# Ten closing transfers regrouped into seven in a decode layer bound by loads

## The chip, the cores and the metric

The kernel runs on one core of one Trainium2 chip. The metric is device microseconds of one execution, the median of the runs shown. A profiled execution gives the trace, all of whose times are microseconds from the start of its span.

## The reference

One token of width D = 640 goes through attention over a cache of 8192 positions in 32 heads of width 192, and then a gated feed-forward layer of width 1536. All numbers are float32. Cut to what matters:

```python
def _A_ref(x, k_cache, v_cache, wq, wo):
    q = (x @ wq).reshape(B, Sq, H, Dh)                      # heads in front
    scores = jnp.einsum("bhqd,bhkd->bhqk", q, k_cache) * (Dh ** -0.5)
    p = _softmax(scores, axis=-1)
    o = jnp.einsum("bhqk,bhkd->bhqd", p, v_cache)
    return o.reshape(B, Sq, H * Dh) @ wo

def _B_ref(x, W_gate, W_up, W_down):
    gate, up = x @ W_gate, x @ W_up
    gate = gate * (gate > 0)
    return (gate * up) @ W_down

h = x + _A_ref(_layernorm(x), k_cache, v_cache, wq, wo)
out = h + _B_ref(_layernorm(h), W_gate, W_up, W_down)
```

## The kernel before

**Layout.** The host packs the inputs so that each transfer is one long row for each of 128 partitions. `kk[h]` is one head's K: 12288 columns of 4 bytes (`KW`). `vv[h]` is one head's V in twelve blocks of 1024 columns, then that head's output weights (960 columns, `WO`), then the next head's query weights (960 columns, `WQ`); 14208 columns in all (`VW`). The last head's V and output weights, without query weights, are `v0`. The feed-forward weights are `ww`: up (7680 columns), gate (7680) and down (7680).

On the chip one tensor, `big`, holds a single K buffer `kt`, two V buffers `vts[0]` and `vts[1]`, and the five columns of x. The feed-forward weights are laid over K and the first V buffer, starting at column 0, once those are free.

**Order of the loads.** All large loads are issued by SP (`sync_fn`), on one queue that the sixteen DMA engines drain in order. For each head, K (line 133) waits for the semaphore `sp`, counted when the scores of the head before are done. V (line 138) waits for `wo`, counted when the output projection that reads the buffer is done. The two then alternate in a loop. The last head is written out by hand: K in two halves with semaphores `k` and `k2`, V in two pieces (line 154), seven blocks on `vb` and five blocks with the output weights on `vb1`. Then come waits for `wo` and `sp` of the last head, and six feed-forward pieces (line 158), cut at the columns in `CUTS`: up; three fifths of gate; the rest of gate with two of down's twelve blocks; six blocks; three blocks; one block.

**One head.** In `tensor_fn`, TensorE computes the query (five pairs of matmuls over the query weights), waits for K, and computes the scores with 24 matmuls for each half of K: the program's 12 float32 matmuls are each two in the trace. A wait for `k2` stands between the halves. For all heads but the last SP raises `k2` ahead of time. Then `output` projects the head before, whose V is already weighted. VectorE takes the maximum of the scores, ScalarE the exponential, TensorE the sums (tile `pl`), VectorE their reciprocal. After that VectorE multiplies the twelve V blocks by the weights and sums them, one custom operation of 1024 columns each (line 126); in the second head of each loop pass it waits for `vb1` before block number `JV` = 7. In the middle of the twelve it also extracts the next query's two columns.

**The end.** `tensor_end` projects the last head, and the layer norm of the sum gives `hc`, the operand of up and gate. `project` runs up (40 traced matmuls) and gate (40), all into tile `sp`. Before gate's fourth block of rows it runs an idle matmul of 256 columns that computes nothing used. ScalarE scales up's result, VectorE multiplies it with the positive part of gate and transposes it (`guT`), while TensorE runs two more idle matmuls. Then come the 96 traced matmuls of down, into `pq`, a copy by ScalarE (line 340), and two small stores. `weights` puts a wait for a piece's semaphore in front of the first matmul that reads at one of the cuts.

Of the kernel before, what the change touches and what calls it, by code (L numbers as in the profile page):

```python
# [10 lines left out]
P, Q, NQ = 128, 32, 4  # L11
H, S, DH, D, F = 32, 8192, 192, 640, 1536
DJ, FJ = D // P, F // P
NG = 8
C = P // NG
SG = S // NG
NJ = DH // C
QB = 512
# [3 lines left out]
DG, FG, HN = D // NQ, F // NQ, D // 2  # L22
KW = S + S // 2
WO = D + HN
WQ = DJ * DH
VW = KW + WO + WQ
JV = 7
GATE, DOWN, FW = DJ * F, 2 * DJ * F, 2 * DJ * F + FJ * D
CUTS = (0, GATE, GATE + 3 * F, DOWN + 2 * D, DOWN + 8 * D, DOWN + 11 * D, FW)
SCALE = DH ** -0.5  # L30
EPS = 1e-5

# [24 lines left out]


def mha_decode_reglu_kernel(nc, x, w0, kk, vv, v0, ww, out):
    names = ("xr", "k", "k2", "va", "vb", "vb1", "qd", "qs", "sp", "mp", "pt", "m1", "rs",  # L60
             "pl", "q", "op", "po", "o", "o2", "wo", "cst", "st", "ffn0", "ffn1", "ffn2", "ffn3", "ffn4",
             "ffn5", "h4", "hm", "hc", "hr", "pu", "us", "pg", "gu", "pd", "pool", "dve")
    stored, s_o4 = (nc.alloc_semaphore("e_" + n) for n in ("out", "o4"))
    s = {n: nc.alloc_semaphore("e_" + n) for n in names}
    nums = sorted(x.num for x in s.values())
# [2 lines left out]
    def sb(name, shape):  # L68
        return nc.alloc_sbuf_tensor(name, shape, F32).ap()
# [1 line left out]
    def ps(name, shape):  # L71
        return nc.alloc_psum_tensor(name, shape, F32).ap()

    big = sb("big", [P, KW + 2 * VW + DJ])
    kt, vt2 = big[:, 0:KW], big[:, KW:]
    vts = [vt2[:, i * VW:(i + 1) * VW] for i in range(2)]
    xrow = sb("xrow", [NQ, DG])
    quad = sb("quad", [NQ, P])
    ones = sb("ones", [P, P])
# [40 lines left out]
    po = ps("po", [P, QB])  # L120
    acc = ps("acc", [P, QB])

    xT = vt2[:, 2 * VW:2 * VW + DJ]

    def ttr(eng, dst, a, b, scale, res):
        return eng.tensor_tensor_reduce(out=res, in0=a, in1=b, scale=scale, scalar=0.0,  # L126
                                        op0=ALU.mult, op1=ALU.add, accum_out=dst)

    def sync_fn(sy):
        def load_k(h, n, dst=kt, c=slice(0, KW), sem="k"):  # L130
            if n is not None:
                sy.wait_ge(s["sp"], n)
            sy.dma_start(dst[:, c], kk[h][:, c]).then_inc(s[sem], 16)  # L133

        def load_v(h, n, b):
            if n is not None:
                sy.wait_ge(s["wo"], n)
            sy.dma_start(vts[b], vv[h]).then_inc(s["vb" if b else "va"], 16)

        sy.dma_start(vt2[:, VW + KW + WO:2 * VW + DJ], w0).then_inc(s["vb"], 16)  # L140
        load_k(0, None)
        load_v(0, None, 0)
        sy.sem_inc(s["k2"], 16 * (H - 1))
        sy.sem_inc(s["vb1"], 16 * (H // 2))
        with sy.Fori(1, H - 2, 2) as i:
            load_k(i, i)
            load_v(i, i, 1)
            load_k(i + 1, i + 1)
            load_v(i + 1, i + 1, 0)
        load_k(H - 1, H - 1, c=slice(0, KW // 2))  # L150
        load_k(H - 1, None, c=slice(KW // 2, KW), sem="k2")
        sy.wait_ge(s["wo"], H - 1)
        for c0, c1, n in ((0, JV * SG, "vb"), (JV * SG, KW + WO, "vb1")):
            sy.dma_start(vts[1][:, c0:c1], v0[:, c0:c1]).then_inc(s[n], 16)
        sy.wait_ge(s["wo"], H)
        sy.wait_ge(s["sp"], H)
        for i, (c0, c1) in enumerate(zip(CUTS, CUTS[1:])):
            sy.dma_start(big[:, c0:c1], ww[:, c0:c1]).then_inc(s[f"ffn{i}"], 16)  # L158

    def store(eng, g):  # L160
        rows = out[0].rearrange("o (g n) -> (o g) n", g=NQ)
# [181 lines left out]
    def mm(dst, lhsT, rhs, start, stop, **kw):  # L343
        return nc.tensor.matmul(dst, lhsT, rhs, start=start, stop=stop, **kw)  # L344

    def weights(c0, n):
        if c0 in CUTS:
            nc.tensor.wait_ge(s[f"ffn{CUTS.index(c0)}"], 16)
        return big[:, c0:c0 + n]

    def project(c0, w0, done):
        for j in range(DJ):
            if w0 + j * F == CUTS[2]:
                idle(QB // 2)
            for g in range(NQ):
                ins = mm(sp[g * Q:(g + 1) * Q, c0:c0 + FG], hc[:, j, :], weights(w0 + j * F + g * FG, FG),
                         j == 0, j == DJ - 1)
            if j == 0 and c0 == 0:
                nc.tensor.wait_ge(s["st"], 8)
                mm(pl[:, 0:1], ones, st[:, 10:11], True, True).then_inc(s["st"])  # L360
        ins.then_inc(s[done])
# [15 lines left out]
    def tensor_fn(t):  # L377
        def query(w):
            wq = w.rearrange("p (j n) -> p j n", n=DH)
            for j in range(DJ):  # L380
                ins = mm(pq[:, 0:DH], xn[:, j:j + 1].to_broadcast([P, P]), wq[:, j, :], j == 0, j == DJ - 1)
            ins.then_inc(s["q"])

        def scores():
            for u in range(NU):
                if u:
                    yield
                for k in range(3):
                    for g in range(NQ):
                        c0 = u * (KW // 2) + (k * NQ + g) * QB  # L390
                        ins = mm(sp[g * Q:(g + 1) * Q, u * QB:(u + 1) * QB], qs[:, k, :], kt[:, c0:c0 + QB],
                                 k == 0, k == 2)
            ins.then_inc(s["sp"])
            yield

        def head(i, b, i8):
            n = i + b if b else i
            t.wait_ge(s["va" if b else "vb"], i8)
            query(vts[1 - b][:, KW + WO:VW])
            t.wait_ge(s["qs"], n)  # L400
            sc = scores()
            k_wait(i, b, "k")
            next(sc)
            k_wait(i, b, "k2")
            next(sc)
            output(t, n, vts[1 - b])
            t.wait_ge(s["mp"], n)
            t.transpose(pt[:, 0:P], mp.to_broadcast([P, P]), ident).then_inc(s["pt"])  # L408
            t.wait_ge(s["rs"], n)
            mm(pl[:, 0:1], share, rs, True, True).then_inc(s["pl"])  # L410

        def k_wait(i, b, name):
            t.wait_ge(s[name], i * 16 + 16 * b if b else i * 16)

        t.wait_ge(s["op"], 1)
        t.wait_ge(s["st"], 1)
        mm(pt[:, 0:1], ones, st[:, 4:5], True, True).then_inc(s["st"])
        t.wait_ge(s["xr"], 16)
        mm(acc[:, 0:DG], quad, xrow, True, False, skip_group_check=True)
        t.wait_ge(s["st"], 3)  # L420
        mm(pl[:, 0:1], ones, st[:, 6:7], True, True).then_inc(s["st"])
        t.wait_ge(s["st"], 7)
        with t.Fori(1, H + 1, 2) as i:
            i8 = i * 8 + 8
            head(i, 0, i8)
            head(i, 1, i8)
        t.sem_inc(s["q"], 1)

    def idle(n):
        mm(pt[:, 0:n], ident, p[:, 0:n], True, True)  # L430

    def tensor_end(t):
        output(t, H + 1, vts[1])
        t.wait_ge(s["h4"], 1)
        mm(pt[:, 0:1], ones, hs1, True, True).then_inc(s["hm"])

        t.wait_ge(s["hc"], 1)
        project(0, 0, "pu")
        project(QB, GATE, "pg")
        idle(QB)  # L440
        idle(QB // 2)
        for g in range(NQ):
            mm(pq[g * Q:(g + 1) * Q, 0:DG], ones[g * Q:g * Q + 1, 0:Q], h4[g * Q:g * Q + 1, :], True, False,
               skip_group_check=True)
        t.wait_ge(s["gu"], 1)
        for j in range(FJ):
            for g in range(NQ):
                ins = mm(pq[g * Q:(g + 1) * Q, 0:DG], guT[:, j, :], weights(DOWN + j * D + g * DG, DG),
                         False, j == FJ - 1, skip_group_check=True)
        ins.then_inc(s["pd"])  # L450
# [14 lines left out]
def _pack(x, k, v, wq, wo, up, gate, down):  # L465

    import numpy as _np

    kk = _np.empty((H, P, KW), k.dtype)
    vv = _np.empty((H - 1, P, VW), v.dtype)  # L470
    v0 = _np.empty((P, KW + WO), v.dtype)
    w0 = _np.empty((P, WQ + DJ), v.dtype)
    w = wq.reshape(P, DJ, H, DH)
    o = wo.reshape(H, DH, D)
    w0[:, 0:WQ] = w[:, :, 0, :].reshape(P, WQ)
    w0[:, WQ:] = x.reshape(P, DJ)
    for h in range(H):
        t = k[0, h].T
        kh = kk[h].reshape(P, NU, 3, NQ, QB)
        kh[:, :, 0:2] = t[0:D1].reshape(P, NQ, 2, NU, QB).transpose(0, 3, 2, 1, 4)  # L480
        kh[:, :, 2] = t[D1:].reshape(D2, NQ, 2, NU, QB).transpose(2, 0, 3, 1, 4).reshape(P, NU, NQ, QB)
        r = vv[h] if h < H - 1 else v0
        r[:, 0:KW] = v[0, h].reshape(NG, SG, NJ, C).transpose(0, 3, 2, 1).reshape(P, KW)
        r[:, KW:KW + D] = o[h, 0:D1]
        r[:, KW + D:KW + WO] = o[h, D1:].reshape(D2, 2, HN).transpose(1, 0, 2).reshape(P, HN)
        if h < H - 1:
            r[:, KW + WO:] = w[:, :, h + 1, :].reshape(P, WQ)
    ww = _np.concatenate([a.reshape(P, -1) for a in (up, gate, down)], axis=1)
    return w0, kk, vv, v0, ww


# [21 lines left out]
```

## Time and profile before

| What | Value |
|---|---|
| Median of 3 runs | 1038.33 us (1038.3 to 1038.48) |
| The profiled execution | 1038.14 us |
| Its span, first to last instruction | 1036.9 us |
| TensorE matmuls / VectorE busy | 438.0 us (42%) / 525.2 us (51%) |
| Bytes moved, rate | 445.98 MB, 430 GB/s |
| Mean granted TensorE clock | 0.641 |

A row of a timeline gives the start, the busy time, the engine and line, the operation, the tiles it writes and reads, and in brackets how long the engine had been idle and what released it. Rows that merge several instructions end in their number. The chain of waits is followed back from the last instruction: each row is a stretch of work or a transfer on which the next one waited. A row of windows gives the stretch, its length, TensorE's busy time, its granted clock, the DMA engines' mean busy share and the rate.

### The profile page before, as it was taken

The page shows a single profiled execution, that of the slowest core. Times are in us where ns is not written, and L with a number is a line of the kernel's source. Part 1 is how long each engine was busy: PE and PEld are TensorE (multiplying, and loading weights), DVE is VectorE, ACT ScalarE, POOL GpSimd, SP SyncE. Part 2 cuts the span into 40 slices and gives each one's busy share as a digit, 9 for nine tenths or more (in the row PEclk, how much of TensorE's full clock was granted, in tenths as well). Part 3 has the DMA queues.
Part 4 walks back from the last instruction along what each step waited for, and adds up shares of the span by engine and source line. Part 5 has one row for each costly group of instructions (what it writes and reads, how often), then busy time and mean ns, then how long its engine had stood idle before and what let it go on. Part 6 is the DMA issues. An engine that isn't in the chain of part 4 may idle for free.

```text
span 1036.9 us, 7438 instructions
## 1 busy us (share of the span) xinstructions
PE 438.0 (42%) x2746; PEld 201.2 (19%) x2746; DVE 525.2 (51%) x1162; ACT 74.5 (7%) x174; POOL 2.8 (0%) x18
## 2 busy tenths in 40 slices
PE   4255343344443344443443443443433553433536
PEld 2122121122121121111221111221211221211203
DVE  1644465644555544556544556444656444656472
ACT  1000000000000000000000000000000000000001
POOL 1000000000000000000000000000000000000000
PEclk8566666666655666655666655666656666656667
DMA  9999999999999999999999999999999999999998
GB/s 402 450 423 432 432 427 449 420 428 432 434 449 420 449 430 432 432 420 451 419 432 432 431 449 420 427 434 436 446 420 451 423 432 432 424 451 420 427 435 346
DMA packets 10532, 445.98 MB, mean 430 GB/s; under 512 B 1176, under 2 KB 1184, under 8 KB 1568
## 3 DMA queue, kind: packets, MB, share of 16 engines
q1 hardware_dynamic: 10516, 445.92, 99.6%
q8 instruction: 3, 0.05, 0.0%
q14 instruction: 1, 0.01, 0.0%
q10 hardware_dynamic: 12, 0.00, 0.0%
HBM read 445.91 MB, written 0.00 MB: 430 GB/s over the span
## 4 chain that ended last, share of the span: by engine, by line
DMA 76%; PE 23%; issue 0%; SPq 0%; DVE 0%; ACT 0%
DMA big<-in_kk_dram 72%; PE sp L344 23%; DMA big<-in_ww_dram 3%; SPq L133 0%; SPq L158 0%; PE pq L344 0%; PE acc L344 0%; SPq L140 0%; DVE junk L126 0%; PE po L344 0%; ACT o L340 0%; DVE o L126 0%
## 5 line engine op out<-in xcount | busy, mean ns | idle before, releaser
L126 DVE CUSTOM_DVE_ANT_0 big<-big,p 128x1024 f32<-128x1024 f32 x384 | 444.9, 1220 | 146.5 <-DMA big<-in_vv_dram 145.3
L344 PE MATMUL sp<-big,qs 128*32 128x512 f32 x1536 | 239.9, 789 | 342.9 <-DMA big<-in_kk_dram 338.4
L344 PE MATMUL pq<-big,xn 128*128 128x192 f32 x320 | 113.4, 540 | 154.2 <-DMA big<-in_vv_dram 152.3
L344 PEld LDWEIGHTS sp<-big,qs 128*32 128x32 f32 x1536 | 55.9, 140 | 513.4 <-DMA big<-in_kk_dram 359.7
L126 DVE CUSTOM_DVE_ANT_0 junk<-blk,po,rl 128x8 f32<-128x8 f32 x66 | 11.9, 218 | 265.5 <-PE po L344 265.5
L344 PEld LDWEIGHTS pq<-big,xn 128*128 128x128 f32 x320 | 97.9, 331 | 157.0 <-DMA big<-in_vv_dram 155.0
L303 ACT ACTIVATE o<-side,o 128x64 f32<-128x64 f32 x33 | 11.5, 348 | 479.2 <-DVE o L126 479.2
L315 ACT ACTIVATE qs<-pick,q 128x64 f32<-128x64 f32 x33 | 11.5, 348 | 410.3 <-DVE q L126 410.3
L321 ACT ACTIVATE p<-sp,m 128x1024 f32<-128x1024 f32 x32 | 35.6, 1113 | 47.9 <-DVE m L259 47.9
L257 DVE TENSOR_REDUCE mp<-sp 128x1 f32<-128x1024 f32 x32 | 39.0, 1220 | 0.0
L344 PE MATMUL pl<-rs,share 128*128 128x1 f32 x64 | 16.5, 327 | 51.9 <-ACT p L321 51.9
L261 DVE RECIPROCAL rl<-pl 128x1 f32<-128x1 f32 x32 | 5.4, 169 | 59.0 <-PE pl L344 59.0
L344 PE MATMUL acc<-big,o 128*32 128x160 f32 x528 | 28.8, 316 | 15.3 <-DVE o L126 15.3
L126 DVE DVE_READ_ACCUMULATOR2_ANT op<- 128x1 f32 x384 | 31.4, 82 | 0.0
L344 PEld LDWEIGHTS pl<-rs,share 128*128 128x128 f32 x64 | 13.8, 268 | 58.0 <-ACT p L321 58.0
L344 PE MATMUL po<-op,same 128*128 128x12 f32 x66 | 13.1, 272 | 16.0 <-PEq L452 16.0
L344 PEld LDWEIGHTS po<-op,same 128*128 128x128 f32 x66 | 10.0, 191 | 42.9 <-issue 26.8
L259 DVE TENSOR_REDUCE m<-pt 128x1 f32<-128x128 f32 x32 | 9.3, 292 | 13.3 <-PE pt L408 13.3
L344 PEld LDWEIGHTS acc<-big,o 128*32 128x32 f32 x528 | 10.6, 108 | 25.8 <-DVE o L126 18.4
L408 PE MATMUL pt<-ident,mp 128*128 128x128 f32 x32 | 10.3, 323 | 8.9 <-DVE mp L257 8.9
L126 DVE CUSTOM_DVE_ANT_0 junk<-ident,pq 128x128 f32<-128x128 f32 x33 | 9.3, 282 | 3.7 <-PE pq L344 3.7
L316 ACT ACTIVATE qs<-pick,q 128x32 f32<-128x32 f32 x33 | 10.1, 307 | 0.0
(78 smaller groups left out, 73.8 us busy)
## 6 DMA issues: line engine op xcount, KB each, us to landing
big<-in_vv_dram SPq DMA_DIRECT2D x31, 7104.0 KB, 38.8
big<-in_kk_dram SPq DMA_DIRECT2D x31, 6144.0 KB, 23.6
big<-in_kk_dram SPq DMA_DIRECT2D x2, 3072.0 KB, 19.5
big<-in_ww_dram SPq DMA_DIRECT2D x1, 3840.0 KB, 20.3
big<-in_v_dram SPq DMA_DIRECT2D x1, 3584.0 KB, 30.2
big<-in_v_dram SPq DMA_DIRECT2D x1, 3040.0 KB, 37.1
big<-in_ww_dram SPq DMA_DIRECT2D x1, 2304.0 KB, 25.5
big<-in_ww_dram SPq DMA_DIRECT2D x1, 2176.0 KB, 30.2
```

The source lines that it names most:

```text
L126: return eng.tensor_tensor_reduce(out=res, in0=a, in1=b, scale=scale, scalar=0.0, op0=ALU.mult, op1=ALU.add, accum_out=dst)
L257: v.reduce_max(mp, sp, axis=AX.X).then_inc(s["mp"])
L259: v.reduce_max(m1, pt[:, 0:P], axis=AX.X, negate=True).then_inc(s["m1"])
L261: v.reciprocal(rl, pl[:, 0:1])
L303: a.mul(o2, side, o[:, 1:2]).then_inc(s["o2"])
L315: a.mul(qs[:, 0:2, :], pk[:, 0:2, :], q[:, 0:1])
L316: a.mul(qs[:, 2, :], pk[:, 2, :], q[:, 1:2]).then_inc(s["qs"])
L321: a.activation(p, sp, AF.Exp, bias=m1, accum_out=rs).then_inc(s["rs"])
L344: return nc.tensor.matmul(dst, lhsT, rhs, start=start, stop=stop, **kw)
L408: t.transpose(pt[:, 0:P], mp.to_broadcast([P, P]), ident).then_inc(s["pt"])
```

## The change

The last head's K comes whole, on `k`; `k2` and its waits are gone from every head. V's first piece is ten blocks. Its second piece, on `vb1`, is two blocks, the output weights and all of up, and it is issued after a wait for the last head's scores, since its columns reach into K's place. For that the buffers change places in `big`: V1, the columns of x padded to 16, K, V0. What is left of the feed-forward weights comes in four pieces, placed behind up, over the rest of K and over V0: gate with two down blocks; six blocks; three; one. The idle matmul inside `project` is gone. The bytes in total are the same.

```diff
-JV = 7
-GATE, DOWN, FW = DJ * F, 2 * DJ * F, 2 * DJ * F + FJ * D
-CUTS = (0, GATE, GATE + 3 * F, DOWN + 2 * D, DOWN + 8 * D, DOWN + 11 * D, FW)
+JV = 10
+XW = 16
+UP = DJ * F
+VL = KW + WO + UP
+GATE, DOWN, FW = 0, DJ * F, DJ * F + FJ * D
+CUTS = (0, DOWN + 2 * D, DOWN + 8 * D, DOWN + 11 * D, FW)
...
-    big = sb("big", [P, KW + 2 * VW + DJ])
-    kt, vt2 = big[:, 0:KW], big[:, KW:]
-    vts = [vt2[:, i * VW:(i + 1) * VW] for i in range(2)]
+    big = sb("big", [P, VW + XW + KW + VW])
+    xT, kt = big[:, VW:VW + DJ], big[:, VW + XW:VW + XW + KW]
+    vts = [big[:, VW + XW + KW:], big[:, 0:VW]]
+    upw, ffn = big[:, KW + WO:VL], big[:, VL:VL + FW]
...
-        sy.sem_inc(s["k2"], 16 * (H - 1))
...
-        load_k(H - 1, H - 1, c=slice(0, KW // 2))
-        load_k(H - 1, None, c=slice(KW // 2, KW), sem="k2")
+        load_k(H - 1, H - 1)
         sy.wait_ge(s["wo"], H - 1)
-        for c0, c1, n in ((0, JV * SG, "vb"), (JV * SG, KW + WO, "vb1")):
-            sy.dma_start(vts[1][:, c0:c1], v0[:, c0:c1]).then_inc(s[n], 16)
+        sy.dma_start(big[:, 0:JV * SG], v0[:, 0:JV * SG]).then_inc(s["vb"], 16)
+        sy.wait_ge(s["sp"], H)
+        sy.dma_start(big[:, JV * SG:VL], v0[:, JV * SG:VL]).then_inc(s["vb1"], 16)
         sy.wait_ge(s["wo"], H)
-        sy.wait_ge(s["sp"], H)
         for i, (c0, c1) in enumerate(zip(CUTS, CUTS[1:])):
-            sy.dma_start(big[:, c0:c1], ww[:, c0:c1]).then_inc(s[f"ffn{i}"], 16)
+            sy.dma_start(ffn[:, c0:c1], ww[:, c0:c1]).then_inc(s[f"ffn{i}"], 16)
...
-        return big[:, c0:c0 + n]
+        return ffn[:, c0:c0 + n]
...
-            if w0 + j * F == CUTS[2]:
-                idle(QB // 2)
             for g in range(NQ):
-                ins = mm(sp[g * Q:(g + 1) * Q, c0:c0 + FG], hc[:, j, :], weights(w0 + j * F + g * FG, FG),
-                         j == 0, j == DJ - 1)
+                n = j * F + g * FG
+                ins = mm(sp[g * Q:(g + 1) * Q, c0:c0 + FG], hc[:, j, :], w(n), j == 0, j == DJ - 1)
...
-            sc = scores()
-            k_wait(i, b, "k")
-            next(sc)
-            k_wait(i, b, "k2")
-            next(sc)
+            t.wait_ge(s["k"], i * 16 + 16 * b if b else i * 16)
+            scores()
...
-        project(0, 0, "pu")
-        project(QB, GATE, "pg")
+        project(0, lambda n: upw[:, n:n + FG], "pu")
+        project(QB, lambda n: weights(GATE + n, FG), "pg")
...
-    v0 = _np.empty((P, KW + WO), v.dtype)
+    v0 = _np.empty((P, VL), v.dtype)
...
-    ww = _np.concatenate([a.reshape(P, -1) for a in (up, gate, down)], axis=1)
+    v0[:, KW + WO:] = up.reshape(P, UP)
+    ww = _np.concatenate([a.reshape(P, -1) for a in (gate, down)], axis=1)
```

More of the change, by code (lines that the diff above doesn't have):

```diff
@@ L59, in mha_decode_reglu_kernel @@
 def mha_decode_reglu_kernel(nc, x, w0, kk, vv, v0, ww, out):
-    names = ("xr", "k", "k2", "va", "vb", "vb1", "qd", "qs", "sp", "mp", "pt", "m1", "rs",
-             "pl", "q", "op", "po", "o", "o2", "wo", "cst", "st", "ffn0", "ffn1", "ffn2", "ffn3", "ffn4",
-             "ffn5", "h4", "hm", "hc", "hr", "pu", "us", "pg", "gu", "pd", "pool", "dve")
+    names = ("xr", "k", "va", "vb", "vb1", "qd", "qs", "sp", "mp", "pt", "m1", "rs",
+             "pl", "q", "op", "po", "o", "o2", "wo", "cst", "st", "ffn0", "ffn1", "ffn2", "ffn3",
+             "h4", "hm", "hc", "hr", "pu", "us", "pg", "gu", "pd", "pool", "dve")
     stored, s_o4 = (nc.alloc_semaphore("e_" + n) for n in ("out", "o4"))
@@ L121, in mha_decode_reglu_kernel @@
     acc = ps("acc", [P, QB])
-    xT = vt2[:, 2 * VW:2 * VW + DJ]
     def ttr(eng, dst, a, b, scale, res):
@@ L129, in sync_fn, with load_k @@
     def sync_fn(sy):
-        def load_k(h, n, dst=kt, c=slice(0, KW), sem="k"):
+        def load_k(h, n):
             if n is not None:
                 sy.wait_ge(s["sp"], n)
-            sy.dma_start(dst[:, c], kk[h][:, c]).then_inc(s[sem], 16)
+            sy.dma_start(kt, kk[h]).then_inc(s["k"], 16)
         def load_v(h, n, b):
@@ L138, in load_v @@
             sy.dma_start(vts[b], vv[h]).then_inc(s["vb" if b else "va"], 16)
-        sy.dma_start(vt2[:, VW + KW + WO:2 * VW + DJ], w0).then_inc(s["vb"], 16)
+        sy.dma_start(big[:, KW + WO:VW + DJ], w0).then_inc(s["vb"], 16)
         load_k(0, None)
         load_v(0, None, 0)
-        sy.sem_inc(s["k2"], 16 * (H - 1))
         sy.sem_inc(s["vb1"], 16 * (H // 2))
@@ L348, in weights, with project @@
             nc.tensor.wait_ge(s[f"ffn{CUTS.index(c0)}"], 16)
-        return big[:, c0:c0 + n]
-    def project(c0, w0, done):
+        return ffn[:, c0:c0 + n]
+    def project(c0, w, done):
         for j in range(DJ):
-            if w0 + j * F == CUTS[2]:
-                idle(QB // 2)
             for g in range(NQ):
-                ins = mm(sp[g * Q:(g + 1) * Q, c0:c0 + FG], hc[:, j, :], weights(w0 + j * F + g * FG, FG),
-                         j == 0, j == DJ - 1)
+                n = j * F + g * FG
+                ins = mm(sp[g * Q:(g + 1) * Q, c0:c0 + FG], hc[:, j, :], w(n), j == 0, j == DJ - 1)
             if j == 0 and c0 == 0:
@@ L385, in scores @@
             for u in range(NU):
-                if u:
-                    yield
                 for k in range(3):
@@ L393, in scores @@
             ins.then_inc(s["sp"])
-            yield
         def head(i, b, i8):
@@ L410, in head @@
             mm(pl[:, 0:1], share, rs, True, True).then_inc(s["pl"])
-        def k_wait(i, b, name):
-            t.wait_ge(s[name], i * 16 + 16 * b if b else i * 16)
         t.wait_ge(s["op"], 1)
```

## The prediction

> **What bounds the kernel now.** I read the page first, then the transfers, the chain that ended last, and the timeline of the last 100 us.
>
> ```profile
> DMA  9999999999999999999999999999999999999998
> HBM read 445.91 MB, written 0.00 MB: 430 GB/s over the span
> DMA 76%; PE 23%; issue 0%; SPq 0%; DVE 0%; ACT 0%
> ```
>
> The sixteen DMA engines are busy in every slice but the last. The PE share of the chain is score matmuls during which the value transfer of the same head is still moving, so the body is bound by bytes. The bytes don't change; what the change reorders is the end.
>
> The transfers of the end, and the small first one (KB of one transfer, then us from issue to landing):
>
> ```profile
> big<-in_kk_dram SPq DMA_DIRECT2D x2, 3072.0 KB, 19.5
> big<-in_v_dram SPq DMA_DIRECT2D x1, 3584.0 KB, 30.2
> big<-in_v_dram SPq DMA_DIRECT2D x1, 3040.0 KB, 37.1
> big<-in_ww_dram SPq DMA_DIRECT2D x1, 2176.0 KB, 30.2
> big<-in_ww_dram SPq DMA_DIRECT2D x1, 960.0 KB, 36.2
> big<-in_ww_dram SPq DMA_DIRECT2D x1, 320.0 KB, 36.5
> big<-in_w_dram SPq DMA_DIRECT2D x1, 482.5 KB, 3.5
> ```
>
> and SP's issues in time (start, duration):
>
> ```profile
> 967.93 0.81 SPq L133 DMA_DIRECT2D big<-in_kk_dram  x2
> 969.57 0.80 SPq L154 DMA_DIRECT2D big<-in_v_dram  x2
> 995.80 2.70 SPq L158 DMA_DIRECT2D big<-in_ww_dram  x6
> ```
>
> So the two pieces of the last V land at 969.57 + 30.2 = 999.8 and about 970.0 + 37.1 = 1007.1. Six feed-forward issues share 2.70 us, 0.45 each; the third lands near 996.7 + 30.2 = 1026.9, the fifth at 997.6 + 36.2 = 1033.8, the last at 998.0 + 36.5 = 1034.5. The chain of waits ends on these:
>
> ```profile
> 396.07 8.32 PE sp L344 x48
> 740.64 6.71 PE sp L344 x48
> ...
> 928.60 8.30 PE sp L344 x48
> 959.92 8.00 PE sp L344 x48
> 991.32 2.78 PE sp L344 x24
> 997.60 36.20 DMA big<-in_ww_dram
> 1033.85 1.34 PE pq L344 x32
> 1035.21 0.30 ACT o L340
> ```
>
> The output copy ends at 1035.5, 1.7 us after the next-to-last landing, and the store fills the rest of the span (1036.9). Two chains race there: bytes, and the arithmetic of the last head. The second decides what this change does.
>
> ```profile
> 945.36 1.23 DVE L126 CUSTOM_DVE_ANT_0 big<-big,p 128x1024 f32<-128x1024 f32 x1 [4.07 <-DMA big<-in_vv_dram]
> 976.69 1.23 DVE L126 CUSTOM_DVE_ANT_0 big<-big,p 128x1024 f32<-128x1024 f32 x1 [4.38 <-DMA big<-in_vv_dram]
> 998.38 0.17 DVE L261 RECIPROCAL rl<-pl 128x1 f32<-128x1 f32 x1 [1.71 <-PE pl L344]
> 999.81 1.22 DVE L126 CUSTOM_DVE_ANT_0 big<-big,p 128x1024 f32<-128x1024 f32 x1 [1.26 <-DMA big<-in_v_dram]
> 1011.62 1.22 DVE L126 CUSTOM_DVE_ANT_0 big<-big,p 128x1024 f32<-128x1024 f32 x1
> 1013.92 0.08 DVE L126 DVE_READ_ACCUMULATOR2_ANT op<- 128x1 f32 x1
> ```
>
> VectorE starts the last head's twelve blocks when the first piece lands (999.81, after 1.26 us of waiting) and ends at 1014.00. The block at 1011.62 is the eleventh. Then TensorE:
>
> ```profile
> 984.73 4.91 PE L344 MATMUL sp<-big,qs 128*32 128x512 f32 x24 [4.45 <-ACT qs L316]
> ...
> 1018.71 1.51 PE L344 MATMUL sp<-big,hc 128*32 128x384 f32 x8 [0.59 <-DVE hc L287]
> ...
> 1020.66 5.96 PE L344 MATMUL sp<-big,hc 128*32 128x384 f32 x56
> 1026.55 0.70 PE L344 MATMUL pt<-p,ident 128*128 128x256 f32 x2
> 1027.17 1.50 PE L344 MATMUL sp<-big,hc 128*32 128x384 f32 x16
> ...
> 1030.49 0.75 PE L344 MATMUL pq<-big,guT 128*32 128x160 f32 x16
> 1031.54 1.84 PE L344 MATMUL pq<-big,guT 128*32 128x160 f32 x48 [0.29 <-DMA big<-in_ww_dram]
> 1033.85 1.29 PE L344 MATMUL pq<-big,guT 128*32 128x160 f32 x32 [0.47 <-DMA big<-in_ww_dram]
> ```
>
> Up and gate start at 1018.71 on VectorE's `hc`, not on weights, and the three down groups wait for bytes only 0.29 and 0.47 us. The arithmetic trails the bytes by almost nothing: its slack is those two waits and the idle matmul at 1026.55. The granted clock of these stretches (length, PE busy, clock, DMA share, GB/s):
>
> ```profile
> 985.66:989.08 3.42, 3.42 (x24) 0.50 0.96 411
> 992.49:995.90 3.41, 2.79 (x34) 1.00 1.06 454
> ...
> 1016.38:1019.80 3.42, 1.96 (x16) 0.50 0.98 417
> 1019.80:1023.21 3.41, 3.41 (x22) 0.50 1.01 430
> 1023.21:1026.62 3.41, 3.41 (x45) 1.00 1.00 418
> ```
>
> **The change, part by part.**
>
> *Rate.* V of head 30 lands 16.8 us after that head's K (959.9 to 976.7): 14208 columns of 512 bytes, 433 GB/s. K in halves takes from there to 991.27, 14.6 us or 431 GB/s; the whole K before it 945.3 to 959.9, the same 14.6 to a tenth. I take 432 GB/s for every piece. As a check, the 36288 columns after 991.27 give 43.0 us, so 1034.3, and the trace has 1034.5.
>
> *K whole.* It lands at 991.2, as its second half did; the join is worth 0 to 0.1 us. What goes is the overlap: today 24 of the 48 score matmuls run from 984.73 while the second half moves, and only 2.78 us remain after the landing. Now all 48 follow it, with a PE that has been idle and starts at half clock. Earlier whole heads cost 6.71 to 8.32 us; the last two fall by 0.30, so 7.7. Scores end at 998.9, not 994.1: +4.8. From scores to VectorE's reciprocal stays 4.45 (994.10 to 998.55), so VectorE is ready at 1003.4 (1002.4 to 1004.0).
>
> *V in 10 and 2 blocks.* The ten-block piece is 10240 columns, 5.24 MB, 12.1 us: it lands at 1003.3. VectorE starts there or just after, 3.6 us later than now, and reaches block eleven after 1011.62 - 999.81 = 11.8 us, at 1015.2.
>
> *Up behind the output weights.* The second piece is two blocks, output weights and up: 10688 columns, 5.47 MB, 12.7 us, landing at 1016.0. VectorE's two last blocks wait for all of it, though they need a fifth of its bytes: 0.8 us more. They end at 1016.05 + (1014.00 - 1011.62) = 1018.4, that is **+4.45** on 1014.00. This landing decides even if scores were quicker.
>
> *The wait moved on SP.* The second piece may be issued only when the scores are done, since up lies in K's place. Behind that wait stand its issue, the `wo` wait and four feed-forward issues. Issue at 999.0 (up to 999.6 at the slowest scores); from the small first transfer, 3.5 us less 1.1 us for its bytes, at most 2.4 us pass until it moves, so by 1001.3 to 1002.0, while the first piece occupies the queue until 1003.3. Cost 0; if that cover went, each us late is a us on the +4.45. The `wo` wait ends 1.7 us after the scores (994.10 to 995.80), near 1000.7, far ahead of 1016.
>
> *Gate whole, with two down blocks.* 8960 columns, 10.6 us: 1026.6. Gate is needed about 6 us after up begins, later than 1028. No wait. The remaining pieces land at 1031.2, 1033.5 and 1034.2.
>
> *Removed.* The k2 wait in every head: nothing, the next K is queued behind a V that moves for another 8.7 us (issue 967.93, landing 976.7). The idle matmul between gate blocks: 1027.17 - 1026.55 = 0.6 us less PE work. Two feed-forward issues and one K issue, 0.45 us of SP each: SP idles. The moved addresses: I take 0; the rows show no price, and any they had would be on DMA rate, bounded by the 431 to 433 above, 0.1 us either way.
>
> *The tail.* `hc` follows VectorE's end as now, so up starts at 1018.71 + 4.45 = 1023.16. Up and gate then took 9.96 us (1018.71 to 1028.67), less 0.6 for the idle matmul: 9.3, with 4.5 us of it at half clock (1018.71 to 1023.21). From gate's end to down stays 1.82. Down, without waits, is 0.75 + 1.84 + 1.29 less some 0.1 of counted pipeline ends: 3.8, against 4.65 now (1030.49 to 1035.14). The sum: +4.45 - 0.63 - 0.85 = **+2.97 us**. On the profiled execution's 1038.14 us that is 1041.1. The median of the shown runs lies 0.19 above that execution, which I leave out; against it 1041.1 is +0.27%.
>
> *The clock.* The half-clock part is uncertain. 24 scores took 4.91 us at a clock of 0.50 and 2.78 at 1.00, close to double with the pipeline's end counted in both. Whole heads of 48 spread over 1.6 us (6.71 to 8.32), so the cold stretch varies by 3.2 us between them: about 2.7 to 5.9, if a wholly warm head takes 5.35. The tail's 4.5 lies in the middle; the other ends move the sum by -0.9 and +0.8.
>
> [...]
>
> **The rivals.**
>
> *The bytes still set the end.* Place: the wait before the last down blocks. Gate no longer waits, and if arithmetic kept ahead, the end would follow the last landing at 1034.2 instead of 1034.5: 1037.9. For it: today's chain ends so, and the bytes are the same. Against: it decides only if VectorE's end slips by less than the slack, 0.63 + 0.29 + 0.47 = 1.4 us, with 0.9 more at the best clock: 2.3, and it slips by 4.45. It would take up landing apart from the two V blocks.
>
> *A fixed price per transfer on the queue.* If the 2.4 us that the small transfer shows beyond its bytes were paid by each one in turn, K whole would land 2.4 us sooner and shift the arithmetic with it: 1041.1 - 2.4 = 1038.7, no change. Against: K in two transfers took 14.6 us, K in one 14.6.
>
> [...]
>
> *The queue runs dry.* If the second V piece starts later than 1003.3, because scores meet the coldest clock and the start takes longer than the small transfer shows, its landing, VectorE and the end all slip: at 1 to 2 us, 1042 to 1043. For it: the issue waits for the scores for the first time. Against: 1.3 to 2 us of margin.
>
> **How the numbers follow.** Forecast 1041.1, chance 0.78, own range 1040.2 to 1041.9 by the clock. Bytes still set the end 0.09, fixed price 0.05, dry queue 0.08. The range takes in VectorE not waiting for the second piece (0.85 less, 1039.6 with a middling-to-good clock) and part of a dry queue: 1039.6 to 1042.5. About 0.2%, 2.1 us, is what a measurement can tell from no change: slower means above 1040.4. The clock leaves about a tenth of the forecast below it: slower 0.70 + 0.08 = 0.78; same 0.08 + 0.05 + 0.06 = 0.19; faster 0.03, what is left of the first two rivals.
>
> **What would show it.** Right: K lands near 991, 48 scores follow until 998 to 1000; VectorE starts near 1003.4 and waits some 0.8 us before its eleventh block, which starts at 1016; up starts near 1023; no feed-forward matmul waits for a DMA; the last weights land near 1034.2 while down starts near 1034.3. The chain of waits ends through VectorE and TensorE instead of feed-forward bytes. Wrong: down still waiting for its last pieces, VectorE's end before 1016, or a gap of the DMA between 1000 and 1005.

## The result, and the profile after

The changed kernel takes 1040.98 us (median of 13 runs, 1040.4 to 1041.66); the kernel before took 1038.44 us beside it (13 runs, 1038.23 to 1038.97). The ratio is 1.0025, with a 95% interval of 1.0017 to 1.0033: slower by a quarter of a per cent. The profiled execution's span is 1039.3 us, before 1036.9.

The end of the chain of waits of the changed kernel (start, us, what):

```profile
1018.91 0.59 PE po L344 x2
...
1023.29 1.51 PE sp L344 x8
1024.80 0.52 PE pl L344 x2
1025.31 6.99 PE sp L344 x72
1032.30 1.49 PE pt L344 x4
1033.79 3.85 PE pq L344 x104
1037.66 0.30 ACT o L340
```

Before, the chain ended through the fifth feed-forward transfer; now it runs without a break through the last projection, the norm, up and gate (`sp`), and down (`pq`), and no transfer is in it. The profile follows it back only to 1018.87, just after VectorE's end; what VectorE waited for before that is read from its own timeline below. The last copy starts at 1037.66, not 1035.21.

Its transfers (KB, us from issue to landing):

```profile
big<-in_v_dram SPq DMA_DIRECT2D x1, 5344.0 KB, 16.8
big<-in_v_dram SPq DMA_DIRECT2D x1, 5120.0 KB, 33.4
big<-in_ww_dram SPq DMA_DIRECT2D x1, 4480.0 KB, 25.7
...
big<-in_ww_dram SPq DMA_DIRECT2D x1, 320.0 KB, 31.4
```

and SP's issues:

```profile
970.04 0.34 SPq L153 DMA_DIRECT2D big<-in_v_dram  x1
999.43 0.33 SPq L155 DMA_DIRECT2D big<-in_v_dram  x1
1001.06 2.48 SPq L158 DMA_DIRECT2D big<-in_ww_dram  x4
```

The ten-block piece lands at 970.04 + 33.4 = 1003.4, the piece with up at 999.43 + 16.8 = 1016.2, gate at 1001.06 + 25.7 = 1026.8. The last down block lands near 1034.5, as before. The bytes are as fast as they were (429 GB/s over the span, 430 before). VectorE's timeline shows what is late:

```profile
1003.64 0.17 DVE L261 RECIPROCAL rl<-pl 128x1 f32<-128x1 f32 x1 [1.71 <-PE pl L344]
1003.78 1.23 DVE L128 CUSTOM_DVE_ANT_0 big<-big,p 128x1024 f32<-128x1024 f32 x1
...
1016.21 1.22 DVE L128 CUSTOM_DVE_ANT_0 big<-big,p 128x1024 f32<-128x1024 f32 x1 [0.53 <-DMA big<-in_v_dram]
...
1018.50 0.08 DVE L128 DVE_READ_ACCUMULATOR2_ANT op<- 128x1 f32 x1
```

It starts the last head 4 us later than before, waits 0.53 us for up's transfer before its eleventh block, and ends at 1018.58 against 1014.00. TensorE's timeline gives both ends of this:

```profile
991.39 7.96 PE L344 MATMUL sp<-big,qs 128*32 128x512 f32 x48 [10.97 <-DMA big<-in_kk_dram]
...
1034.12 3.47 PE L344 MATMUL pq<-big,guT 128*32 128x160 f32 x96
```

All 48 score matmuls follow K's landing; all 96 of down run in one row, with no wait for a transfer.

### The profile page after: what moved, and what is told of

Its sections match the earlier page's. It is cut to its first block, busy times and chain, and to the rows that moved or that the text cites. A ratio compares the mean times of both kernels' runs of the same rounds, so it can differ in the third digit from the quotient of the medians.

```text
span 1039.3 us, 7428 instructions
## 1 busy us (share of the span) xinstructions
PE 437.1 (42%) x2744; PEld 201.4 (19%) x2744; DVE 525.2 (51%) x1162; ACT 74.6 (7%) x174; POOL 2.8 (0%) x18
## 6 DMA issues: line engine op xcount, KB each, us to landing
big<-in_v_dram SPq DMA_DIRECT2D x1, 5344.0 KB, 16.8
big<-in_v_dram SPq DMA_DIRECT2D x1, 5120.0 KB, 33.4
big<-in_ww_dram SPq DMA_DIRECT2D x1, 4480.0 KB, 25.7
```

## The experiments

In each pair of times the kernel before ran on the same chip; it came out between 1038.26 and 1038.32, and at 1038.44 beside the changed kernel. Differences from the changed kernel's 1040.98 are between medians of separate sets of runs and are good to some 0.2 us.

**Which part of the regrouping costs.** Three kernels undo one part or both. The first brings the last K in halves again:

```diff
-        load_k(H - 1, H - 1)
+        load_k(H - 1, H - 1, c=slice(0, KW // 2))
+        load_k(H - 1, None, c=slice(KW // 2, KW), sem="k2")
```

> The changed kernel, but the last K again in two halves on two semaphores. Theory (the landing of the second V piece, with up in it, sets VectorE's end): scores end near 994 as before, VectorE starts at the landing of the ten-block piece, near 1003.5, still waits before its eleventh block and ends near 1018.5; the time stays at 1041.0 (1040.4 to 1041.7). Rival (the lost overlap of K and scores is the cost): the time goes back to 1038.4.

Measured: 1041.04 us (1040.59 to 1041.62), ratio 1.0027 [1.0017, 1.0036]. VectorE's timeline in this run:

```profile
998.58 0.17 DVE L263 RECIPROCAL rl<-pl 128x1 f32<-128x1 f32 x1 [1.71 <-PE pl L346]
1003.62 1.23 DVE L128 CUSTOM_DVE_ANT_0 big<-big,p 128x1024 f32<-128x1024 f32 x1 [4.86 <-DMA big<-in_v_dram]
...
1016.26 1.23 DVE L128 CUSTOM_DVE_ANT_0 big<-big,p 128x1024 f32<-128x1024 f32 x1 [0.75 <-DMA big<-in_v_dram]
```

The overlap is back: VectorE is ready at 998.75, within 0.2 us of before. But it then waits 4.86 us for the ten-block piece and 0.75 us for up's. So the second landing sets its end, though the scores were done 5 us sooner. That K comes whole costs nothing while V comes like this. The rows also say which part of V's regrouping delays VectorE: its first block starts 3.81 us later than in the kernel before (1003.62 against 999.81), for the ten-block piece, and only the 0.75 us is up's.

The second keeps K whole, cuts V at seven blocks again and takes up out of V's second piece:

```diff
-JV = 10
+JV = 7
...
-        sy.wait_ge(s["sp"], H)
-        sy.dma_start(big[:, JV * SG:VL], v0[:, JV * SG:VL]).then_inc(s["vb1"], 16)
+        sy.dma_start(big[:, JV * SG:KW + WO], v0[:, JV * SG:KW + WO]).then_inc(s["vb1"], 16)
+        sy.wait_ge(s["sp"], H)
+        sy.dma_start(upw, v0[:, KW + WO:VL]).then_inc(s["upw"], 16)
```

> The changed kernel with K whole, but V in seven blocks, then five blocks with the output weights, then up as a transfer of its own, which alone waits for the scores. Theory: VectorE no longer waits for bytes, but scores end near 999, so it starts near 1003.8 and needs 14.1 us: end 1017.9, 0.6 us sooner than in the changed kernel, 1040.4. Rival (up in front of the two last blocks is the whole cost): 1038.4.

Measured: 1039.64 us (1038.57 to 1040.73, 11 runs), ratio 1.0012 [1.0003, 1.0022]. The gain on the changed kernel is 1.3 us where 0.6 was expected, and the runs spread over 2.2 us. TensorE and, below it, VectorE in the profiled execution, which took 1040.69:

```profile
991.55 8.13 PE L345 MATMUL sp<-big,qs 128*32 128x512 f32 x48 [11.13 <-DMA big<-in_kk_dram]
...
1023.00 1.51 PE L345 MATMUL sp<-big,hc 128*32 128x384 f32 x8 [0.59 <-DVE hc L288]
...
1024.96 7.45 PE L345 MATMUL sp<-big,hc 128*32 128x384 f32 x72
```

```profile
1003.97 0.17 DVE L262 RECIPROCAL rl<-pl 128x1 f32<-128x1 f32 x1 [1.71 <-PE pl L345]
1004.11 1.22 DVE L128 CUSTOM_DVE_ANT_0 big<-big,p 128x1024 f32<-128x1024 f32 x1
```

VectorE no longer waits for bytes: it starts as soon as its reciprocal is done. The scores took 8.13 us here, near the top of the 6.71 to 8.32 seen for whole heads; in the other traces with K whole the last head's took between 6.74 (e5, below) and 7.96 us. With no landing behind them to hide the difference, that spread can go straight into the end, beside the spread of up and gate. The expectation had used the 7.96 us of one trace as if it were the mean. That the quick runs are those with short scores is argued: only one execution was profiled, a slow one, and in it VectorE ends just 0.3 us sooner than in the changed kernel.

The third undoes both:

> K in halves and V as 7 and 5 with up apart; what is left of the change is the new places in SBUF, gate whole and no idle matmul. Theory: VectorE's end is back at 1014.0 and up starts at 1018.7; now gate waits for its whole transfer, near 1026.8, some 2 us after up is done, so gate ends near 1030.2 and down near 1035.7, 0.5 us later than before: 1038.9, up to 1040.3 if the clock falls to 0.50 in that wait. Rival (either undone part alone is the cause and the rest is free): 1038.1 to 1038.4 with no wait at gate.

Measured: 1038.90 us (1038.48 to 1040.83), ratio 1.0009 [1.0, 1.0018]. TensorE's timeline:

```profile
1019.06 1.51 PE L347 MATMUL sp<-big,hc 128*32 128x384 f32 x8 [0.59 <-DVE hc L290]
...
1021.02 4.74 PE L347 MATMUL sp<-big,hc 128*32 128x384 f32 x32
1027.29 3.43 PE L347 MATMUL sp<-big,hc 128*32 128x384 f32 x40 [1.53 <-DMA big<-in_ww_dram]
```

Up starts four us earlier, near its time in the kernel before, so most of the loss is gone. Now gate whole shows its own price: its 40 matmuls wait 1.53 us for one large landing. Nine of the eleven runs lie between 1038.48 and 1039.22. The two at 1040.56 and 1040.83 lie above even the 1040.3 expected for a clock that falls in that wait; neither was profiled, so their cause is open.

The fourth of this group cuts gate in two again:

```diff
-CUTS = (0, DOWN + 2 * D, DOWN + 8 * D, DOWN + 11 * D, FW)
+CUTS = (0, GATE + 3 * F, DOWN + 2 * D, DOWN + 8 * D, DOWN + 11 * D, FW)
```

> As e3 (K in halves, V as 7 and 5, up apart), and gate again in two transfers, three fifths and the rest with two down blocks; what is left of the change is the new places in SBUF and no idle matmul in gate. Theory (what e3 loses is gate's wait for its whole transfer): the wait is gone or below 0.5 us, and the time is that of the kernel before, 1038.1 to 1038.5. Rival (the new places or the missing idle matmul cost the 0.5 us): 1038.9 as e3.

Measured: 1038.26 us beside 1038.26 for the kernel before; eleven of twelve runs lie between 1038.08 and 1038.51, and one at 1048.72, the only one with a mean granted clock of 1.0 (the others have 0.641 to 0.648), is unexplained; it widens the interval to [0.9992, 1.0025]. TensorE waits for bytes where the kernel before did:

```profile
1020.80 7.97 PE L347 MATMUL sp<-big,hc 128*32 128x384 f32 x72
...
1031.75 1.84 PE L347 MATMUL pq<-big,guT 128*32 128x160 f32 x48 [0.41 <-DMA big<-in_ww_dram]
```

So the new places in SBUF and the missing idle matmul cost nothing that shows, and what e3 still lost was gate whole.

**Is it the arithmetic, and its clock?** The next runs add idle matmuls, which compute nothing that is used, to keep up TensorE's granted clock, which in the changed kernel is 0.50 from 1004 to 1027. The first try put twelve behind the end of the block, the part of the program that holds the head loop:

```diff
+        for _ in range(12):
+            idle(QB)
         output(t, H + 1, vts[1])
+        idle(QB)
         t.wait_ge(s["h4"], 1)
         mm(pt[:, 0:1], ones, hs1, True, True).then_inc(s["hm"])
+        idle(QB // 2, pl)
```

> The changed kernel with idle matmuls (12 of 512 columns before the last projection, one after it, one of 256 columns after the sum of h): they compute nothing that is used. Theory (the arithmetic sets the end, and 2.7 to 5.9 us of up and gate run at half clock): up and gate run at full clock and take 6.8 us, not 9; down catches up with its bytes and waits for them again; 1038.6, with a spread below 0.7 us. Rival (the bytes set the end): no change, 1041.0.

Measured: 1051.01 us (1050.29 to 1051.44, four runs), ratio 1.0121 [1.0106, 1.0137], a miss of its own kind:

```profile
1018.92 12.92 PE L344 MATMUL pt<-p,ident 128*128 128x512 f32 x24 [15.30 <-PEq L445]
...
1035.57 0.85 PE L344 MATMUL sp<-big,hc 128*32 128x384 f32 x8
...
1036.66 6.01 PE L344 MATMUL sp<-big,hc 128*32 128x384 f32 x72
```

TensorE stood idle for 15.30 us, released 0.33 us after VectorE's end (1018.59), though these idle matmuls wait for no semaphore of the kernel: in this run what stands behind the block began only after VectorE's end. The idle matmuls therefore came on top, 12.9 us, and the kernel lost 10.0. That most of the added work comes out in the time fits an end set by arithmetic, but so much of it would show in a kernel with a little slack too. Of the 2.9 us that didn't come out, 1.9 are in up and gate, which took 7.1 us from first to last (1035.57 to 1042.67), not 9.0, at a granted clock of 1.00.

The same idle matmuls inside the block, behind the head loop:

> The changed kernel with the twelve idle matmuls placed right behind the head loop on TensorE, so that they run while VectorE weighs the last V (in the run before they stood behind the end of the block and began only after VectorE's end); the two later idle matmuls stay. They compute nothing that is used. Theory: up and gate take about 7 us, not 9, from the same start near 1023; down then waits for its last two transfers again, so the bytes set the end: 1038.4 (1038.0 to 1038.9), spread under 0.8 us. Rival (the later landing of the weights or the place of up costs by itself): stays near 1041.

Measured: 1039.68 us (1039.09 to 1041.1), 1.3 us better than the changed kernel, less than expected, with a wide spread. TensorE in the profiled execution, which took 1040.09:

```profile
1002.50 13.24 PE L344 MATMUL pt<-p,ident 128*128 128x512 f32 x24
1018.89 0.57 PE L344 MATMUL po<-op,same 128*128 128x12 f32 x2 [3.15 <-PEq L445]
...
1021.15 2.08 PE L344 MATMUL pt<-p,ident 128*128 128x512 f32 x2
...
1023.31 1.20 PE L344 MATMUL pl<-p,ident 128*128 128x256 f32 x2
1024.44 1.10 PE L344 MATMUL sp<-big,hc 128*32 128x384 f32 x8
```

The twelve end 3.15 us before the last projection, the granted clock is 0.50 from 1019 to 1025, and the two later ones take 2.08 and 1.20 us at that clock, longer than their gaps: up starts at 1024.44, over a us late. Fourteen, and shorter ones after them:

> The changed kernel with idle matmuls as in e5, but fourteen instead of twelve behind the head loop, so that they last to about 1018 and the clock isn't lost before the last projection, and the two later ones at half their length (256 and 128 columns), so that they fit their gaps at half clock too. They compute nothing that is used. Theory: up starts at 1022.5 to 1023.3 at full clock, takes 7 us with gate, and down waits for its last transfers: 1038.3 to 1038.8 in most runs. Rival (something else than the clock and VectorE's late end keeps the changed kernel back): 1039.5 or more, as e5.

Measured: 1040.81 us (1039.91 to 1041.21), no gain, and a time that the rival allowed. Windows of TensorE (length, busy, clock, DMA share, GB/s) in the profiled execution, the quickest of the ten:

```profile
1016.40:1019.82 3.42, 1.06 (x11) 0.97 1.14 493
1019.82:1023.23 3.41, 3.41 (x26) 0.50 0.95 410
1023.23:1026.65 3.42, 3.42 (x26) 0.53 0.88 367
```

The last projection starts at 1018.71. The granted clock is 0.97 in the row in which it stands, 0.50 in every us from 1020 to 1026, and 0.77 in the next, while up runs from 1022.88. So the clock that this run was to hold was lost, and it doesn't decide between the theory and its rival. Sixteen, with the later ones as in the first try:

> The changed kernel with sixteen idle matmuls of 512 columns behind the head loop, so that they last beyond VectorE's end (which may delay the last projection by up to 0.7 us), then one of 512 and one of 256 columns as in e4, which kept the clock. They compute nothing that is used. Theory: up and gate run at full clock in 7 us, as in e4 after its late start, and start at 1022.5 to 1023.7; gate's end moves from 1032.3 to near 1030.2, and down waits for its last transfers or nearly: 1038.3 to 1039.2. Rival (the time does not follow the clock of up and gate): 1040.5 or more.

Measured: 1039.40 us (1038.98 to 1040.04), ratio 1.0010 [1.0001, 1.0019]:

```profile
1002.63 16.77 PE L344 MATMUL pt<-p,ident 128*128 128x512 f32 x32
1019.69 0.36 PE L344 MATMUL po<-op,same 128*128 128x12 f32 x2 [0.30 <-PEq L445]
...
1023.66 0.85 PE L344 MATMUL sp<-big,hc 128*32 128x384 f32 x8
...
1024.76 6.01 PE L344 MATMUL sp<-big,hc 128*32 128x384 f32 x72
```

Here the granted clock is 1.00 in every window from 1016.4 to 1036, up and gate take 7.1 us (1023.66 to 1030.77), and the time falls by 1.6 us though the idle matmuls overran VectorE's end and delayed the projection by 0.8 us (1019.69 against 1018.91). Gate ends 1.5 us sooner than in the changed kernel, and the time follows it. The expected 1038.3 to 1039.2 is missed by 0.2 us; the overrun was to be 0.7 us at most, but that it is the reason isn't shown. Down's 96 matmuls still run in one row, with no wait for a transfer, so the arithmetic sets the end here too: with the clock held, what is left of the loss, 1.1 us beside the kernel before, goes with up's start at 1023.66 instead of 1018.71.

The same idle matmuls as in the second try, in the kernel before:

> The kernel before with the same idle matmuls as e5. Theory (its end is set by bytes, with the arithmetic just ahead): 1038.2, at most 0.2 us better, and a smaller spread. Rival (the arithmetic still counts in the kernel before): 1037 or less.

Measured: 1038.29 us beside 1038.29, runs from 1038.19 to 1038.64:

```profile
1027.03 1.50 PE L344 MATMUL sp<-big,hc 128*32 128x384 f32 x16 [0.61 <-DMA big<-in_ww_dram]
...
1031.64 1.84 PE L344 MATMUL pq<-big,guT 128*32 128x160 f32 x48 [0.54 <-DMA big<-in_ww_dram]
1033.96 1.29 PE L344 MATMUL pq<-big,guT 128*32 128x160 f32 x32 [0.48 <-DMA big<-in_ww_dram]
```

The arithmetic is quicker in part: gate's first three blocks end at 1025.79 instead of 1026.62, though up starts 1.3 us later. Only the waits for bytes grow (0.61 before the rest of gate, where there was none, and 0.54 against 0.29 before down's second group). The kernel before is bound by bytes to its end; the changed one is not.

**The two rivals about transfers.** The second V piece is issued after the exponential instead of the scores:

```diff
-        sy.wait_ge(s["sp"], H)
+        sy.wait_ge(s["rs"], H)
```

> The changed kernel, but the second V piece waits for the exponential of the last head instead of its scores: it is issued near 1003.2, not 999.4, just as the first piece lands (1003.5). Theory of the dry queue: the transfer begins 1 to 2.4 us after its issue, so the landing, VectorE and the end slip by 0.8 to 2.2 us: 1041.8 to 1043.2. Rival (an issue costs nothing as long as it is made before the last landing): 1041.0.

Measured: 1042.49 us (1041.92 to 1043.16), ratio 1.0042 [1.0028, 1.0055], 1.5 us above the changed kernel. SP's issue and VectorE's two starts:

```profile
1002.50 0.33 SPq L155 DMA_DIRECT2D big<-in_v_dram  x1
```

```profile
1003.37 1.22 DVE L128 CUSTOM_DVE_ANT_0 big<-big,p 128x1024 f32<-128x1024 f32 x1
...
1017.87 1.23 DVE L128 CUSTOM_DVE_ANT_0 big<-big,p 128x1024 f32<-128x1024 f32 x1 [2.60 <-DMA big<-in_v_dram]
```

Issued 3.1 us later (0.7 us sooner than expected), the piece lands 1.7 us later (1017.87 against 1016.21). If each us of delay costs a us once the margin is used up, the changed kernel's issue had a margin of some 1.4 us. In windows of one us the engines moved 82 GB/s and then 0 between 1001 and 1003 in this run, 597 and 214 in the changed kernel: the queue ran dry here and not there.

Last, three more transfers in the kernel before, up in four parts:

```diff
-            sy.dma_start(big[:, c0:c1], ww[:, c0:c1]).then_inc(s[f"ffn{i}"], 16)
+            n = (c1 - c0) // (4 if i == 0 else 1)
+            for c in range(c0, c1, n):
+                sy.dma_start(big[:, c:c + n], ww[:, c:c + n]).then_inc(s[f"ffn{i}"], 16)
```

> The kernel before, with up in four transfers of 1920 columns on one semaphore instead of one: three more transfers of the same bytes. Theory (a transfer more costs the queue next to nothing): 0 to 0.1 us each, 1038.4 to 1038.7. Rival (each pays a fixed 2 to 2.4 us): 1044.4 to 1045.6.

Measured: 1038.52 us beside 1038.29, ratio 1.0003 [0.9994, 1.0012]: 0.08 us for each transfer, not clear of zero and, by the upper end of the interval, at most 0.4. Joining transfers had little to save here.

No version tried beats the kernel before by more than can be measured.

## Why the prediction was right

The forecast was 1041.1 us by VectorE's late end; 1040.98 was measured. The steps:

| Step | Forecast | Trace after |
|---|---|---|
| K whole lands | 991.2 | 991.4 |
| Scores | 7.7 us | 7.96 us |
| First V piece lands | 1003.3 | 1003.4 |
| Second V piece lands | 1016.0 | 1016.2 |
| VectorE's end moves | +4.45 us | +4.58 us |
| Up starts | 1023.16 | 1023.29 |
| Up and gate | 9.3 us | 9.0 us |
| Down | 3.8 us | 3.5 us |

The steps held in order. The second landing decides, as forecast ("even if scores were quicker"), and K's lost overlap adds nothing to it: e1 showed this directly. VectorE's wait for it was 0.53 us, not 0.8, since the scores ended later. The 7.7 us for them came from letting the last two heads' 8.30 and 8.00 fall once more; in traces with K whole they took 6.74 to 8.13 us, so that this step came so near is partly luck, and it didn't decide. What the prediction didn't price is each part without the other. Beside the kernel before, the changed kernel loses 2.5 us, with K undone 2.7, with V undone 1.3, with both undone 0.6: each of the two can hold back VectorE by itself, so a sum of separate prices would have gone wrong.

Two terms were a little long, up and gate and down, 0.3 us each. For the first, the granted clock is 0.50 in every us from 1019 to 1027 and 0.79 in the next, so half clock lasted to about 1027.4, an estimate: 4.1 us of up and gate, not the 4.5 carried over. The step to full clock came 4.2 us later than in the trace before (1023.21), while up started 4.6 us later. For the second, a row holds some 0.2 us once, however many its matmuls, an estimate from rows of `pq`: 16 took 0.75 us, 48 took 1.84 and 96 took 3.47, or 0.034 us for each further one. Three rows in a sum hold it three times: 3.88 us became 3.47, 0.4 less where 0.1 was taken off. The 5.35 us for a wholly warm head fits twice the 2.78 us of 24 scores less 0.2 of this kind; no whole head was measured so, and the shortest took 6.71. In the profiled execution the sum is +4.58 - 0.95 - 1.18 = +2.45 us, against +4.45 - 0.63 - 0.85 = +2.97 forecast. That the median comes within 0.1 us of 1041.1 is luck: the profiled execution took 1040.59 us, 0.5 less than forecast for it, and the median of the 13 runs is 0.4 us above that execution; between the medians the loss is 2.54 us. The own range of the forecast, 1040.2 to 1041.9 by the clock, holds all 13 runs. Its working has two small slips that change nothing: 1016.05 + 2.38 - 1014.00 is 4.43, not 4.45, and the upper end of the clock moves the sum by 0.7, not 0.8.

The costs put at nothing: gate whole was free, as said, but only because up began late; e3 shows 1.53 us of wait, some 0.6 us of time, once it doesn't, and e10 gets both back. The moved wait on SP was free with some 1.4 us to spare (e6). The idle matmul and the new places cost nothing that shows (e10). The waits for `k2` in every head are back in e1, which takes as long as the changed kernel; the last K lands at 991.4 without them and at 991.27 in the kernel before.

The rivals: bytes no longer set the end (e11, and the chain after). The fixed price is 0.08 us a transfer, at most 0.4 by the interval, not 2.4 (e7); the 2.4 is what the small first transfer took beyond its bytes, and no run shows the 2 at the low end of e7's rival. The queue did run dry in e6 (0 GB/s from 1002 to 1003), but that began some 1.4 us beyond this change.

## What to carry to other kernels

In a kernel like this one, bound by bytes in its body, the end is a race between the last bytes and the arithmetic that follows them: list what each late step needs of its transfer, don't make its first piece longer than the step can wait for (3.8 us of VectorE's delay in e1), and don't put bytes that are needed later into the transfer that an earlier step waits for (0.75 us). Joining large transfers on a queue that was not empty saved next to nothing here (three transfers more cost 0.08 us each in e7), and took away the overlap that the cut gave. Price joined edits together: here undoing one part alone gave nothing, and undoing the other gave half.

## What the runs showed of the hardware

Three things had not been expected. TensorE's instructions behind the block's end started only 0.3 us after VectorE's last one (e4), so here work meant to fill that wait had to stand inside the block. The granted clock was 0.50 in each of the six us from 1020 to 1026 in e9, in all of which TensorE is recorded as busy throughout; in the kernel before it was 0.50 in four such us, from 1019 to 1023, and 0.90 in the next. So how long TensorE ran without a break at 0.50 differed between runs; what sets it isn't shown. And some of SP's issues can take long:

```profile
995.83 9.32 SPq L160 DMA_DIRECT2D big<-in_ww_dram  x9
```

Nine took 9.32 us in e7, against 2.70 us for six in the kernel before. The seventh was issued near 998.6, by its landing (1031.7, 33.1 us after its issue): the first six took some 2.8 us, about as before, and the last three some 6.6 us, an estimate. Why isn't shown. It cost nothing that shows: the last was issued by 1005.15, while the last V was still landing until about 1007.
